# Chunk attention with a split-precision FFN: steps of the attention issued apart, spread evenly, new orders for tiles 2 and 3, aligned pools

## The chip, the cores and the metric

The kernel runs on one core of a Trainium2 chip. Its metric is the device time of one execution in microseconds (us). TensorE (PE) multiplies, VectorE (DVE) and ScalarE (ACT) do elementwise work and reductions, GpSimd (POOL) does some elementwise work too, and the queue of SyncE (SP) issues almost all DMAs. Each engine works through its own instructions in the order in which they were issued and waits on semaphores for the others.

## The reference

Attention within chunks of 64 positions for 8 x 8 heads of 576 positions of 64 features, then a layer norm, a feed-forward network with a ReLU, and a residual:

```python
def _attn_ref(q, k, v):                    # q, k, v: 8, 8, 576, 64
    q_c = q.reshape(B, H, nc, chunk, D)    # chunk = 64, nc = 9; k_c, v_c likewise
    scores = scale * np.matmul(q_c, k_c.transpose(0, 1, 2, 4, 3))
    scores = scores - np.max(scores, axis=-1, keepdims=True)
    attn = np.exp(scores)
    attn = attn / (np.sum(attn, axis=-1, keepdims=True) + 1e-09)
    return np.matmul(attn, v_c)

def _moe_ref(x, g_ln, w_ch1, w_ch2):       # x: 8, 576, 512; w_ch1: 512 x 2048; w_ch2: 2048 x 512
    mu = np.mean(x, axis=-1, keepdims=True)
    var = np.mean((x - mu) ** 2, axis=-1, keepdims=True)
    xn = (x - mu) / np.sqrt(var + 1e-06) * g_ln
    ch = np.maximum(xn @ w_ch1, 0.0) @ w_ch2
    return (x + ch).astype(np.float32)
```

All inputs are float32. The weights of the network reach the chip as 64-bit words and are rounded there.

## The kernel before

**Tokens.** The 4608 tokens form 18 pairs of 2 x 128 tokens, and two pairs form a tile of 512. Tiles 0 to 2 lead; tiles 3 to 8 are taken two at a time, in three units of 1024 tokens. Every wide product is made of three float32r products of a high and a low part (h and l), which stand in for float32: high by high, high by low, low by high.

**Attention of a pair** (`attention`) is a generator. Each `next` issues one step: load q and k, scores on TensorE into the one buffer of the pool `ps_a`, row maxima (`top`) and the load of v, subtraction (VectorE) and exp (ScalarE), four groups of 32x32 transposes on VectorE, denominators, the out product, scaling to x, statistics for the norm and its power -0.5 on POOL, the centred and weighted `xg` with its scaling by `rstd` on ScalarE, four groups of transposes into `rows`. With `by_pe` the transposes run on TensorE through a `ps_a` buffer. `p_sb`, `pt_sb`, `xg` take turns in two buffers of the pool `work`.

**Leading tiles** use the plain network (`ffn`): 16 features groups, each with a run of 12 matmuls up (`u`) and 12 down, a ReLU on ScalarE (`hh`) and its rest on VectorE (`hl`) between (`1`). The order for tile 1 and tile 2 is written out by hand: `SECOND` and `THIRD` give, for each position of the network's run, letters whose generators are stepped ahead of it. A and B are the pairs of tile 2, C and G those of tile 3, D and H those of tile 4, S the preparation of the weights' sums and parts for the units (POOL, ScalarE, DMAs to DRAM), P and Q the operands of the first unit for C with D and for G with H (`combine`), R the start of the ring of weight buffers.

**A unit** (`unit_ffn`) multiplies up by a seven-product scheme of sums: in each of four quarters 14 products of 6 matmuls, with snapshots copied by ScalarE (`snap`) and sums added by VectorE (`hu`), 336 matmuls in all. Then it multiplies down in two halves of 16 runs of 12 matmuls, 384 in all, each run with a relu (`hh` or `hx`) and a rest (`hl` or `hx`) of a later part. Two of five places of these parts lie in the pool `hp`, three (`hx`) in the pool `raws`. While units 0 and 1 run, `weave` steps the attention of the next unit's four pairs: after each `yield n` of the unit it counts n matmuls on and issues every side step that is due. The due counts come from `PAIR_SPAN`, `LOADED` and `STEPS` for the pairs and from `FIRST_HALF`, `LAST_HALF`, `ONE_STEP` for the operands of the next unit.

Nothing is reordered by a scheduler (`manual_schedule`): what is issued first stands first in its engine's queue. The joint step on which the prediction rests most:

```python
            nc.vector.tensor_tensor(out=p_b, in0=s4, in1=top4, op=ALU.subtract)
            nc.scalar.activation(p_sb, p_sb, AF.Exp, scale=scale)
        yield
```

Of the kernel before, what the change touches and what calls it, by code (L numbers as in the profile page):

```python
# [8 lines left out]
F32 = mybir.dt.float32  # L9
# [5 lines left out]
ALU = mybir.AluOpType  # L15
AX = mybir.AxisListType

P = 128
# [7 lines left out]
HP = H // 2  # L26
# [28 lines left out]
FIRST_HALF = 345  # L55
LAST_HALF = 585
REST = (2, 6, 12, 28)
# [34 lines left out]
def quad(i):  # L92
    return slice(32 * i, 32 * i + 32)
# [3 lines left out]
def chunk_attention_ffn(ctx: ExitStack, tc: tile.TileContext, qkv, v01, g, w, out):  # L97
# [9 lines left out]
    small = ctx.enter_context(tc.tile_pool(name="small", bufs=4))  # L107
    raws = ctx.enter_context(tc.tile_pool(name="raws", bufs=1))
# [8 lines left out]
    mhalf = const.tile([P, 2], F32, name="mhalf")  # L117
    nc.gpsimd.memset(mhalf, -0.5)
# [138 lines left out]
    def attention(pair, xt_cols, xs, by_pe, den_by_pe, rows_of=None):  # L257
# [60 lines left out]
        if den_by_pe:  # L318
            for h2 in range(2):
                nc.tensor.matmul(  # L320
                    s2[:, h2, :], lhsT=minus.bitcast(F32), rhs=top4[:, h2], start=False, stop=True,
                    skip_group_check=True,
                )
            nc.scalar.activation(p_b, s4, AF.Exp, scale=scale)
        else:
            nc.vector.tensor_tensor(out=p_b, in0=s4, in1=top4, op=ALU.subtract)  # L326
            nc.scalar.activation(p_sb, p_sb, AF.Exp, scale=scale)  # L327
# [5 lines left out]
        pt_sb = work.tile([P, groups, 2, D], F32, name="pt_sb", tag="work")  # L333
# [99 lines left out]
        for j in range(2):  # L433
            nc.vector.scalar_tensor_tensor(  # L434
                out=xg[:, j, :], in0=x[:, j, :], scalar=mv[:, j, 0:1], in1=g_sb, op0=ALU.subtract, op1=ALU.mult
            )
            if rows_of:
                nc.scalar.activation(xg[:, j, :], xg[:, j, :], AF.Copy, scale=rstd[:, j : j + 1])  # L438
        yield

        if rows_of:
            rows_t = rows_of()
            if by_pe:
                xt = halves()
                for j in range(2):
                    for k in range(NK):
                        ks = slice(k * P, (k + 1) * P)
                        nc.tensor.transpose(out=xt[j][:, ks], in_=xg[:, j, ks], identity=ident)
                    nc.scalar.copy(rows_t[:, :, j * P : (j + 1) * P], xt[j].rearrange("p (k t) -> p k t", k=NK))
                    yield  # L450
            else:
                to = rows_t.rearrange("p k (j t) -> p j k t", j=2)
                of = xg.rearrange("p j (k t) -> p j k t", k=NK)
                for j in range(4):
                    for i in range(4):
                        for h2 in range(2):
                            nc.vector.transpose(  # L457
                                out=to[quad(j), h2, :, quad(i)], in_=of[quad(i), h2, :, quad(j)]
                            )
                    yield  # L460
            return
# [242 lines left out]
    def rows_of(i):  # L704
        if "rows" not in shared:
            shared["rows"] = [xtp.tile([P, NK, 2 * PAIR], F32, name="rows", tag=f"xt{c}") for c in "hl"]
        return shared["rows"][i // 2][:, :, i % 2 * PAIR : (i % 2 + 1) * PAIR]
# [6 lines left out]
    def combine(half):  # L714
        cs = slice(half * PAIR, (half + 1) * PAIR)
        a, b = (r[:, :, cs] for r in shared["rows"])
        b11, b21, b12, b22 = a[:, :2], a[:, 2:], b[:, :2], b[:, 2:]

        def part(name, x):
            o = operand(name)  # L720
            nc.scalar.copy(o[:, 0, :, cs], x)  # L721
            nc.gpsimd.tensor_tensor(out=o[:, 1, :, cs], in0=x, in1=o[:, 0, :, cs].bitcast(F32), op=ALU.subtract)  # L722
# [24 lines left out]
        part("4", b21)  # L747
        yield

    def unit_ffn(u):  # L750
# [22 lines left out]

        def add(out, bank, s):
            nc.vector.tensor_tensor(out=out, in0=bank, in1=s, op=ALU.add)  # L775
# [5 lines left out]
        def split(i):  # L781
# [6 lines left out]
            nc.scalar.activation(hh, x, AF.Relu)  # L788
# [3 lines left out]
            parts.append((hh, hl))  # L792

        for q in range(NF // 4):
# [8 lines left out]

            for e in range(2):
                w0, w1 = pair_of()
                product(c_[e], w0, "2", True)
                yield 6
                product(a_[e], w1, "1", True)
                ring.fetch()
                nc.scalar.copy(s[e][0], a_[e])  # L810
                add(h[e][:, 0, 0], c_[e], s[e][0])
                yield 6
            for e in range(2):
                w0, w1 = pair_of()
                product(a_[e], w0, "6", False)
                nc.scalar.copy(s[e][1], a_[e])
                yield 6
                product(c_[e], w1, "5", True)
                ring.fetch()
                nc.scalar.copy(s[e][2], c_[e])  # L820
                yield 6
            for e in range(2):
                w0, w1 = pair_of()
                product(a_[e], w0, "7", False)
                add(h[e][:, 1, 1], a_[e], s[e][2])
                yield 6
                product(c_[e], w1, "3", False)
                ring.fetch()
                add(h[e][:, 1, 0], c_[e], s[e][1])
                if q == NF // 4 - 1:  # L830
                    split(e)
                yield 6
            w01 = pair_of()
            for e in range(2):
                product(a_[e], w01[e], "4", False)
                if e == 1:
                    ring.fetch()
                nc.scalar.copy(h[e][:, 0, 1], a_[e])  # L838
                yield 6
# [7 lines left out]
        for n in range(2):  # L847
# [3 lines left out]
            def down(f, w, j, m):  # L851
                hh, hl = (x[:, j * P : (j + 1) * P] for x in parts[n * NF + f])
# [7 lines left out]
            for f in range(NF):  # L860
                ws[f] = ring.take()[:, : 2 * DM].rearrange("p (h n) -> p h n", h=2)
                if f < NF - 2:
                    for m, j in [(m, j) for j in range(4) for m in range(3)] if f == 0 else [
                        (m, j) for m in range(3) for j in range(4)
                    ]:
# [10 lines left out]
                    yield 12  # L876
            for j in range(4):
                for f in range(NF - 2, NF):
                    for m in range(3):
                        down(f, ws[f], j, m)  # L880
                pair, jj = pairs[j // 2], j % 2
# [7 lines left out]
                if j == 3:  # L889
                    ring.fetch()  # L890
                    ring.fetch()
                    for f in range(NF - 2, NF):
                        if n * NF + f + ahead < 2 * NF:
                            split(n * NF + f + ahead)
                yield 6
# [18 lines left out]
    class Tokens:  # L914
# [10 lines left out]
        def attention(self, i, by_pe=False, den_by_pe=False):  # L925
# [3 lines left out]
            return attention(2 * self.t + i, lambda: self.cols(i), xs, by_pe, den_by_pe, rows)  # L929
# [14 lines left out]
    with tc.manual_schedule():  # L944
# [4 lines left out]
            G=tiles[3].attention(1), H=tiles[4].attention(1, True), S=prepare(), R=start_ring(), P=combine(0), Q=combine(1),  # L949
# [60 lines left out]
```

## Time and profile before

| | |
|---|---|
| median of three runs | 879.55 us (878.25 to 879.68) |
| the profiled execution | 880.14 us, of which the span of instructions is 878.3 us |
| mean granted clock of TensorE | 0.992 |
| busy: TensorE, VectorE, ScalarE, POOL | 843.6, 569.8, 270.3, 150.0 us |
| HBM | 147.08 MB read, 39.85 MB written |

The profile gives for every instruction its start, its length, the idle time of its engine before it and what ended that idle time. In its lines a group stands as line, engine, operation, written tile <- read tiles, shapes and count. In the order of time, a line begins with start and length in us, and the idle time before it with its releaser stands in brackets. The chain that ended last is the path, followed back from the last instruction, of what released what. Matmuls overlap, so the time that one takes in a run is the distance from start to start, not its own length of about 390 ns.

### The profile page before, as it was taken

Reading aid. Unit: us, or ns where it says so; the run is one execution under the profiler, and the core shown is the slowest. Engines: PE = TensorE matmul, PEld = TensorE weight load, DVE = VectorE, ACT = ScalarE, POOL = GpSimd, SP = SyncE. Lnnn points to the kernel's source line nnn. Section 1 sums busy time; section 2 is a strip of 40 time slices with the busy share of each in tenths; the row PEclk is TensorE's granted clock in tenths of the full one; section 3 lists DMA queues with packets and bytes.
Section 4 is the critical chain, followed back from the end, with each engine's and each line's share of the span. In section 5 each row is a group of like instructions: output and inputs, shape, how many; then the busy total and the mean of one; then the engine's idle time right before and its main releaser. Section 6 shows DMA issues by size and latency. Waiting matters only on the chain.

```text
span 878.3 us, 14775 instructions
## 1 busy us (share of the span) xinstructions
PE 843.6 (96%) x5850; PEld 686.8 (78%) x5850; DVE 569.8 (65%) x1101; ACT 270.3 (31%) x425; POOL 150.0 (17%) x138
## 2 busy tenths in 40 slices
PE   7999999999898899999998999999989999999998
PEld 4888888887677688878886888778868888888886
DVE  6989947567837734788987846879888622132321
ACT  5766321122322322232422412234322212232220
POOL 0110024473811122100120220001301300000000
PEclk9999999999999999999999999999999999999999
DMA  9996509948861046776783769767756776666573
GB/s 356 325 294 165 193 0 333 334 161 276 273 215 66 0 168 229 229 242 216 236 316 138 271 195 324 243 209 251 240 188 219 238 240 192 194 195 234 192 261 119
DMA packets 69044, 192.60 MB, mean 219 GB/s; under 512 B 6640, under 2 KB 20976, under 8 KB 67056
## 3 DMA queue, kind: packets, MB, share of 16 engines
q1 hardware_dynamic: 67680, 186.95, 62.7%
q0 software_dynamic: 1296, 4.72, 2.8%
q8 instruction: 46, 0.75, 0.3%
q14 instruction: 22, 0.18, 0.1%
HBM read 147.08 MB, written 39.85 MB: 213 GB/s over the span
## 4 chain that ended last, share of the span: by engine, by line
PE 75%; DVE 14%; issue 6%; DMA 2%; ACT 2%; POOL 1%; SPq 0%; ACTq 0%; POOLq 0%; DVEq 0%
PE y L769 22%; PE y L853 19%; PE y L543 11%; PE h L519 11%; PE h L853 8%; DVE rows L457 3%; DVE pt_sb L349 2%; PE s L294 1%; PE h L378 1%; DMA wp<-wfs 1%; DVE xg L434 1%; DVE p_sb L326 1%; DVE hu L775 1%; DVE stats L422 1%; DVE xt L492 1%
## 5 line engine op out<-in xcount | busy, mean ns | idle before, releaser
L769 PE MATMUL y<-xc,ring 128*128 128x512 f32 x1008 | 233.2, 391 | 2.7 <-ACT hu L838 2.0
L769 PEld LDWEIGHTS y<-xc,ring 128*128 128x128 f32 x1008 | 188.1, 188 | 43.9 <-ACT hu L838 2.8
L853 PE MATMUL y<-ring,hx 128*128 128x512 f32 x486 | 132.6, 400 | 1.5 <-ACT hx L788 1.5
L519 PE MATMUL h<-xth,wp 128*128 128x512 f32 (+1 forms) x432 | 130.1, 372 | 1.3 <-DMA wp<-wfs 1.3
L853 PEld LDWEIGHTS y<-ring,hx 128*128 128x128 f32 x486 | 91.6, 190 | 24.0 <-ACT hx L788 2.3
L775 DVE TENSOR_TENSOR hu<-y,snap 128x512 f32<-128x512 f32 x72 | 48.8, 688 | 82.9 <-ACT snap L810 50.8
L543 PE MATMUL y<-wp,hh 128*128 128x512 f32 x376 | 96.3, 394 | 0.0
L519 PEld LDWEIGHTS h<-xth,wp 128*128 128x128 f32 x432 | 79.0, 190 | 16.1 <-DMA wp<-wfs 1.5
L722 POOL TENSOR_TENSOR xc<-rows,xc 128x512 fp32r<-128x512 f32 x42 | 57.5, 1382 | 146.2 <-ACT xc L721 143.1
L349 DVE STREAM_TRANSPOSE pt_sb<-p_sb 32x256 f32<-32x256 f32 x176 | 76.7, 436 | 6.6 <-ACT p_sb L327 2.3
L543 PEld LDWEIGHTS y<-wp,hh 128*128 128x128 f32 x376 | 69.4, 189 | 14.0
L533 DVE SCALAR_TENSOR_TENSOR hl<-h,hh 128x512 fp32r<-128x512 f32 (+1 forms) x53 | 33.0, 628 | 72.4 <-ACT hh L532 71.9
L519 PE MATMUL h<-xtl,wp 128*128 128x512 f32 (+1 forms) x216 | 78.8, 369 | 0.0
L457 DVE STREAM_TRANSPOSE rows<-xg 32x128 f32<-32x128 f32 x288 | 71.6, 282 | 4.1 <-ACT xg L438 2.0
L853 PE MATMUL y<-ring,hh 128*128 128x512 f32 x252 | 71.8, 395 | 0.0
L789 DVE SCALAR_TENSOR_TENSOR hx<-hu,hx 128x512 fp32r<-128x512 f32 x54 | 41.7, 790 | 40.0 <-ACT hx L788 14.6
L532 ACT ACTIVATE hh<-h 128x512 fp32r<-128x512 f32 (+1 forms) x53 | 28.5, 545 | 106.6 <-PE h L519 102.3
L853 PEld LDWEIGHTS y<-ring,hh 128*128 128x128 f32 x252 | 47.7, 190 | 11.2 <-DVE hu L775 0.6
L543 PE MATMUL y<-wp,hl 128*128 128x512 f32 x188 | 51.8, 389 | 0.0
L853 PE MATMUL h<-ring,hx 128*128 128x512 f32 x162 | 50.9, 395 | 0.0
L428 POOL TENSOR_TENSOR rstd<-vare,mhalf 128x2 f32<-128x2 f32 x12 | 10.8, 901 | 230.3 <-DVE vare L427 230.3
L788 ACT ACTIVATE hx<-hu 128x512 fp32r<-128x512 f32 x54 | 33.1, 628 | 48.9 <-PE y L853 29.8
(129 smaller groups left out, 1005.1 us busy)
## 6 DMA issues: line engine op xcount, KB each, us to landing
ring<-w2d SPq DMA_DIRECT2D x96, 512.0 KB, 4.2
ring<-wa SPq DMA_DIRECT2D x84, 512.0 KB, 4.3
raw<-w SPq DMA_DIRECT2D x15, 1024.0 KB, 7.4
out<-x SPq DMA_DIRECT2D x36, 256.0 KB, 4.4
q_t<-qkv SPq DMA_DIRECT2D x17, 512.0 KB, 6.1
k_t<-qkv SPq DMA_DIRECT2D x17, 512.0 KB, 6.9
v_t<-qkv SPq DMA_DIRECT2D x32, 256.0 KB, 6.8
w2d<-wp SPq DMA_DIRECT2D x16, 512.0 KB, 7.3
```

What stands on the lines that cost most here:

```text
L349: nc.vector.transpose(out=pt_sb[quad(2 * h2 + j), :, c, quad(i)], in_=p_sb[quad(2 * c + i), :, h2, quad(j)])
L457: nc.vector.transpose(out=to[quad(j), h2, :, quad(i)], in_=of[quad(i), h2, :, quad(j)])
L519: nc.tensor.matmul(h, lhsT=(wh, wh, wl)[m][:, ks], rhs=(xth, xtl, xth)[m][:, k, :], start=i == 0, stop=i == len(terms) - 1,)
L532: nc.scalar.activation(hh, h, AF.Relu)
L533: nc.vector.scalar_tensor_tensor(out=hl, in0=h, scalar=0.0, in1=hh.bitcast(F32), op0=ALU.max, op1=ALU.subtract)
L543: nc.tensor.matmul(sums(pairs[j // 2])[j % 2], lhsT=(hh, hh, hl)[m], rhs=(wh, wl, wh)[m], start=f == 0 and m == 0, stop=f == NF - 1 and m ...
L722: nc.gpsimd.tensor_tensor(out=o[:, 1, :, cs], in0=x, in1=o[:, 0, :, cs].bitcast(F32), op=ALU.subtract)
L769: nc.tensor.matmul(bank, lhsT=w[:, (0, 0, 1)[m], ks], rhs=x[:, (0, 1, 0)[m], k, :], start=start and k == m == 0, stop=k == 1 and m == 2, s ...
L775: nc.vector.tensor_tensor(out=out, in0=bank, in1=s, op=ALU.add)
L788: nc.scalar.activation(hh, x, AF.Relu)
L789: nc.vector.scalar_tensor_tensor(out=hl, in0=x, scalar=0.0, in1=hh.bitcast(F32), op0=ALU.max, op1=ALU.subtract)
L853: nc.tensor.matmul(ys[j], lhsT=(hh, hh, hl)[m], rhs=w[:, (0, 1, 0)[m]], start=f == 0 and m == 0, stop=f == NF - 1 and m == 2,)
```

## The change

- Subtraction and exp become two steps where the rows go to a unit, and so do `xg` and its scaling. In the unit, relu (`split`) and rest (`rest`) are issued at different places within a run, a run of 12 matmuls yields three times instead of once, and in the product stage the side steps are issued ahead of a product's fetch, copies and adds instead of behind them.
- `rows` is laid out by token half first, so that a group of transposes is 4 of 32x256 instead of 8 of 32x128; `combine` reads and writes it with strides.
- `STEPS` has 18 entries for 16, `PAIR_SPAN` is 140 for 138; `SECOND`, `THIRD`, `ROOMS` and `REST` are new. H's `pt_sb` lies in the pool `raws`.
- `mhalf` is 128 bytes wide instead of 8, and a pool of 64 bytes lies ahead of `raws`.

```diff
 SECOND = {
-    0: "ABS", 1: "AS", 2: "AS", 3: "AS", 4: "A", 5: "AS", 6: "AS", 7: "ABS", 8: "AS", 9: "AC", 10: "AS", 11: "AS",
-    12: "AS", 13: "AS", 14: "A", 15: "AS", 16: "BS", 17: "BS", 18: "BS", 19: "B", 20: "BS", 21: "BS", 22: "BS",
-    23: "BCS", 24: "BC", 25: "BBS", 26: "BS", 27: "BBS", 28: "BBS", 29: "CD", 30: "CCS", 31: "CS", 32: "C",
+    0: "ABS", 1: "AS", 2: "S", 3: "AAS", 4: "AS", 5: "AAS", 6: "S", 7: "AS", 8: "AAS", 9: "AAS", 10: "AAS", 11: "BAS",
+    12: "BAC", 13: "BS", 14: "S", 15: "BBS", 16: "BS", 17: "BBS", 18: "S", 19: "BS", 20: "BBCS", 21: "BBS", 22: "BBDS",
+    23: "BCS", 24: "BC", 25: "CS", 26: "S", 27: "CCS", 28: "CS", 29: "CCS", 30: "CDS", 31: "CDDS", 32: "DS",
 }
 THIRD = {
-    0: "CDS", 1: "CDS", 2: "DGS", 3: "CS", 4: "CDDS", 5: "DS", 6: "DS", 7: "DG", 8: "DG", 9: "GH", 10: "DGG", 11: "DGG",
-    12: "GP", 13: "GHP", 14: "GHP", 15: "GGP", 16: "GGHP", 17: "GGP", 18: "P", 19: "HHP", 20: "HP", 21: "HHP", 22: "HP",
-    24: "H", 25: "H", 26: "QQ", 27: "QQR", 28: "Q", 29: "QXXN", 30: "QR",
+    0: "CS", 1: "CS", 2: "DDG", 3: "D", 4: "DD", 5: "D", 6: "DG", 7: "GGH", 8: "DG", 9: "D", 10: "GGP", 11: "HGP",
+    12: "GGP", 13: "GHP", 14: "GGHP", 15: "GHP", 16: "GP", 17: "HHGP", 18: "HGG", 19: "HGP", 20: "HP", 21: "HP",
+    22: "H", 24: "H", 25: "H", 26: "QQ", 27: "QR", 28: "Q", 29: "QXXN", 30: "QQR", 31: "Q",
 }
-ROOMS = {1: (3, 11), 2: (6,)}
-PAIR_SPAN = 138
+ROOMS = {1: (3, 9), 2: (6,)}
+PAIR_SPAN = 140
-STEPS = (0, 8, 16, 30, 40, 50, 60, 70, 80, 87, 95, 105, 116, 126, 136, 146)
-ONE_STEP = 8
+STEPS = (0, 6, 11, 18, 26, 37, 48, 59, 68, 76, 88, 95, 102, 110, 118, 129, 140, 158)
+ONE_STEP = 9
-LAST_HALF = 585
-REST = (2, 6, 12, 28)
+LAST_HALF = 592
+REST = (2, 6, 20)
...
+    gap = ctx.enter_context(tc.tile_pool(name="gap", bufs=1))
+    gap.tile([P, 16], F32, name="gap")
     raws = ctx.enter_context(tc.tile_pool(name="raws", bufs=1))
...
-    mhalf = const.tile([P, 2], F32, name="mhalf")
+    halves_ = const.tile([P, 32], F32, name="mhalf")
+    mhalf = halves_[:, :2]
...
             nc.vector.tensor_tensor(out=p_b, in0=s4, in1=top4, op=ALU.subtract)
+            if rows_of:
+                yield
             nc.scalar.activation(p_sb, p_sb, AF.Exp, scale=scale)
...
-            if rows_of:
+        yield
+        if rows_of:
+            for j in range(2):
                 nc.scalar.activation(xg[:, j, :], xg[:, j, :], AF.Copy, scale=rstd[:, j : j + 1])
-        yield
+            yield
...
-                to = rows_t.rearrange("p k (j t) -> p j k t", j=2)
-                of = xg.rearrange("p j (k t) -> p j k t", k=NK)
+                to = rows_t.rearrange("p j k t -> p (j k) t")
+                of = xg.rearrange("p j (k t) -> p (j k) t", k=NK)
                 for j in range(4):
                     for i in range(4):
-                        for h2 in range(2):
-                            nc.vector.transpose(
-                                out=to[quad(j), h2, :, quad(i)], in_=of[quad(i), h2, :, quad(j)]
-                            )
+                        nc.vector.transpose(out=to[quad(j), :, quad(i)], in_=of[quad(i), :, quad(j)])
                     yield
...
             nc.scalar.activation(hh, x, AF.Relu)
+            parts.append((hh, hl, x))
+
+        def rest(i):
+            hh, hl, x = parts[i]
             nc.vector.scalar_tensor_tensor(
...
+            for i, (bank, e, name, then) in enumerate(steps):
+                if i % 2 == 0:
+                    w01 = pair_of()
+                product(bank[e], w01[i % 2], name, name in "215")
                 yield 6
+                if i % 2:
                     ring.fetch()
+                if then:
+                    then(e)
+                if q == NF // 4 - 1 and name in "34":
+                    (split if name == "3" else rest)(e)
...
                         down(f, ws[f], j, m)
+                        if at % 4 == 3:
+                            yield 4
+                            if at == 3 and n == f == 0:
+                                rest(2)
+                            if at == 3 and f > 0 and i - 1 < 2 * NF:
+                                split(i - 1)
+                            if at == 7 and f > 0 and i - 1 < 2 * NF:
+                                rest(i - 1)
                     ring.fetch()
-                    if n * NF + f + ahead < 2 * NF:
-                        split(n * NF + f + ahead)
...
+                yield 6
                 pair, jj = pairs[j // 2], j % 2
                 x = back[pair][:, jj, :]
                 nc.vector.tensor_tensor(out=x, in0=ys[j], in1=x, op=ALU.add)
...
+                if n == 0 and j < 3:
+                    split(NF + j)
+                    rest(NF + j)
```

`then` holds the copies and adds of a product as before (`copy` and `add`; the products keep their order), and `i` in the down stage is the number of the part three runs ahead.

More of the change, by code (lines that the diff above doesn't have):

```diff
@@ L255, in unspill, with attention @@
         return x
-    def attention(pair, xt_cols, xs, by_pe, den_by_pe, rows_of=None):
+    def attention(pair, xt_cols, xs, by_pe, den_by_pe, rows_of=None, pt_raw=False):
         if pair == 1:
@@ L331, in attention @@
             nc.gpsimd.memset(v_1.rearrange("p j a b d -> p (j a b) d")[:, :, D:], 1.0)
-        pt_sb = work.tile([P, groups, 2, D], F32, name="pt_sb", tag="work")
+        if pt_raw:
+            pt_sb = raws.tile([P, groups, 2, D], F32, name="pt_raw", tag="wf")
+        else:
+            pt_sb = work.tile([P, groups, 2, D], F32, name="pt_sb", tag="work")
         if by_pe:
@@ L772, in product, with copy @@
                     )
+        def copy(out, bank):
+            nc.scalar.copy(out, bank)
         def add(out, bank, s):
@@ L802, in pair_of @@
                 return w[:, 0], w[:, 1]
+            steps = []
             for e in range(2):
-                w0, w1 = pair_of()
-                product(c_[e], w0, "2", True)
-                yield 6
[L808 to L836, printed above, removed]
+                steps += [
+                    (c_, e, "2", None),
+                    (a_, e, "1", lambda e: (copy(s[e][0], a_[e]), add(h[e][:, 0, 0], c_[e], s[e][0]))),
+                ]
@@ new lines, in unit_ffn @@
+            for e in range(2):
+                steps += [
+                    (a_, e, "6", lambda e: copy(s[e][1], a_[e])),
+                    (c_, e, "5", lambda e: copy(s[e][2], c_[e])),
+                ]
+            for e in range(2):
+                steps += [
+                    (a_, e, "7", lambda e: add(h[e][:, 1, 1], a_[e], s[e][2])),
+                    (c_, e, "3", lambda e: add(h[e][:, 1, 0], c_[e], s[e][1])),
+                ]
+            for e in range(2):
+                steps += [(a_, e, "4", lambda e: copy(h[e][:, 0, 1], a_[e]))]
@@ L851, in down @@
             def down(f, w, j, m):
[L852 removed]
+                hh, hl = (x[:, j * P : (j + 1) * P] for x in parts[n * NF + f][:2])
                 nc.tensor.matmul(
@@ L888, in unit_ffn @@
                     stores.append((out[row : row + P, :], x))
[L889 to L895, printed above, removed]
+                if n == 0 and j < 3:
+                    split(NF + j)
+                    rest(NF + j)
+            ring.fetch()
+            ring.fetch()
         for to, of in stores:
```

34 lines of the change are left out of this document (16 added, 18 removed).

## The prediction

> **What bounds the kernel now.** I read the page first, then the busy times by stage (the stages are cut where the chain that ended last goes from one loop to the next), the chain itself, and the order of time on TensorE, ScalarE and VectorE around each gap.
>
> ```profile
> PE 843.6 (96%) x5850; PEld 686.8 (78%) x5850; DVE 569.8 (65%) x1101; ACT 270.3 (31%) x425; POOL 150.0 (17%) x138
> ```
> ```profile
> 0.00:132.00 132.00, 124.12 (x1147) 101.76 (x1147) 106.21 (x153) 72.06 (x97) 13.73 (x24) 1.00 0.68 222
> 132.00:218.00 86.00, 86.00 (x619) 71.24 (x616) 58.24 (x109) 18.49 (x26) 44.02 (x40) 1.00 0.82 282
> 218.00:342.00 124.00, 112.38 (x910) 91.44 (x909) 72.94 (x136) 34.28 (x57) 42.41 (x37) 0.97 0.43 150
> ...
> 526.00:710.00 184.00, 178.27 (x1232) 143.88 (x1232) 143.88 (x321) 53.00 (x90) 23.52 (x18) 0.99 0.70 235
> 710.00:875.00 165.00, 164.56 (x719) 134.64 (x717) 43.73 (x65) 38.47 (x64) 0.00 (x0) 1.00 0.64 208
> ```
>
> Columns behind the stretch and its length: busy time of PE, PEld, DVE, ACT, POOL, then granted clock, DMA share, GB/s. TensorE is the bound, so only its idle time, its clock and the time between its matmuls can be won. The stage of tile 1 (132 to 218) has no idle time. The stage of tile 2 (218 to 342) has 124 - 112.38 = 11.62 us of it at a clock of 0.97. A unit with attention beside it (526 to 710; the unit ahead of it is like it) has 184 - 178.27 = 5.73 us at 0.99. The last unit, with no side work, has nearly none.
>
> The chain gives the price of a clean unit:
>
> ```profile
> 525.55 2.72 PE y L769 x12
> 528.26 1.09 PE s L294 x64
> 529.36 17.91 PE y L769 x78
> ...
> 709.74 76.16 PE y L769 x336
> 785.90 45.71 PE y L853 x198
> ...
> 874.60 0.69 DVE x L883
> ```
>
> Unit 2 runs from 525.55 to 709.74, 184.2 us; unit 3, with the same 720 wide matmuls, to 874.60, 164.9 us. Four pairs of attention add eight blocks of 64 small matmuls; a block takes 1.09 and makes the run behind it 17.91 - 78 x 0.2267 = 0.23 longer, so 8 x 1.32 = 10.6. The other 184.2 - 164.9 - 10.6 = 8.7 us of a unit are waits and what follows from them.
>
> These are the waits of unit 2, in order of time on TensorE, with the granted clock around the worst:
>
> ```profile
> 566.61 5.74 PE L769 MATMUL y<-xc,ring 128*128 128x512 f32 x24 [0.38 <-DVE hu L775]
> 573.33 1.90 PE L769 MATMUL y<-xc,ring 128*128 128x512 f32 x7 [0.98 <-ACT hu L838]
> 646.94 5.86 PE L853 MATMUL y<-ring,hx 128*128 128x512 f32 x24 [0.76 <-ACT hx L788]
> 656.14 0.30 PE L378 MATMUL h<-v_t,pt_sb 64*64 64x64 f32 x2 [3.07 <-DVE pt_sb L349]
> 656.97 1.50 PE L378 MATMUL h<-v_t,pt_sb 64*64 64x64 f32 x58 [0.54 <-DVE pt_sb L349]
> ```
> ```profile
> 646.00:666.00 20.00, 15.63 (x117) 12.27 (x117) 16.26 (x32) 4.24 (x8) 0.00 (x0) 0.91 0.34 113
> ```
>
> They add up to the 5.73. And what stood in front, on ScalarE and VectorE:
>
> ```profile
> 569.23 1.22 DVE L301 TENSOR_REDUCE top<-s 128x16 f32<-128x1024 f32 x1
> 570.49 1.22 DVE L326 TENSOR_TENSOR p_sb<-s,top 128x1024 f32<-128x1024 f32 x1
> 573.80 0.69 DVE L775 TENSOR_TENSOR hu<-y,snap 128x512 f32<-128x512 f32 x1 [2.08 <-ACT snap L810]
> ```
> ```profile
> 571.75 1.06 ACT L327 ACTIVATE p_sb<-p_sb 128x1024 f32<-128x1024 f32 x1 [4.90 <-DVE p_sb L326]
> 572.71 0.57 ACT L838 COPY hu<-y 128x512 f32<-128x512 f32 x1
> ...
> 645.31 1.06 ACT L327 ACTIVATE p_sb<-p_sb 128x1024 f32<-128x1024 f32 x1 [8.85 <-DVE p_sb L326]
> 646.28 1.66 ACT L788 ACTIVATE hx<-hu 128x512 fp32r<-128x512 f32 x3
> ```
>
> Subtraction and exp of a pair are issued in one step. ScalarE then stands 4.90 (later 8.85) us at the exp, waiting for a late VectorE, and the copy that frees TensorE's bank, or three relus that make its operands, stand behind it. VectorE in turn waits for those copies (2.08), so its lag lasts, until a pair's out product at 653 finds its transposes missing.
>
> **The change, part by part.** The profiled execution took 880.14 us (span 878.3); the median is 879.55, 0.6 less, and the gain is taken from the median.
>
> *Aligned pools.* In the program as allocated, tiles are rounded up to 32 bytes and pools lie one behind the other; every large tile but those of the pool "raws" starts 32 bytes over a multiple of 128, those of raws 96 over. The wider mhalf (32 to 128 bytes) and the gap of 64 bytes put all of them on multiples of 128. What the 96 costs is seen where the operand's parts lie in raws (hx) and where they don't (hh, hl):
>
> ```profile
> 802.32 1.98 PE L853 MATMUL y<-ring,hh 128*128 128x512 f32 x8
> 804.14 1.07 PE L853 MATMUL y<-ring,hl 128*128 128x512 f32 x4
> 805.04 8.56 PE L853 MATMUL y<-ring,hx 128*128 128x512 f32 x36
> 813.44 1.78 PE L853 MATMUL y<-ring,hh 128*128 128x512 f32 x7
> ```
> ```profile
> 6.05 1.30 PE L235 MATMUL y<-minus 128*128 128x512 f32 x5
> ```
>
> From start to start, hx takes (813.44 - 805.04) / 36 = 233 ns, hh and hl (805.04 - 802.32) / 12 = 227. Over a unit: 45.71 / 198 = 230.9 against 76.16 / 336 = 226.7, so 4.2 ns x 384 = 1.6 us, 4.8 in three units. The value for "all on 128" is not in the main loops; the nearest row is the keep-warm run, where both operands are minus, on a multiple of 128: (1.30 - 0.39) / 4 = 228 with a last matmul of 0.39 as elsewhere, so 227 is not expected to move. Ends: 0 and 4.8. I take 4.8, as the difference follows the pool.
>
> A rule speaks against it: the Trainium skill (SBUF — State Buffer, Specifications) has lines of 16 bytes and a penalty for each new line; 32 and 96 are both multiples of 16, so by it this part gives nothing. The hx row differs all the same.
>
> *Units 1 and 2.* Subtraction and exp, xg and its scaling, relu and its rest become steps 6 to 8 matmuls (1.4 to 1.8 us) apart, so the second engine no longer stands at the first one's queue; a pair gets 140 matmuls for 138, the side steps come ahead of a product's copies instead of behind. The row transposes go from 32 small to 16 larger:
>
> ```profile
> L349 DVE STREAM_TRANSPOSE pt_sb<-p_sb 32x256 f32<-32x256 f32 x176 | 76.7, 436 | 6.6 <-ACT p_sb L327 2.3 <-PE s L448 1.7
> L457 DVE STREAM_TRANSPOSE rows<-xg 32x128 f32<-32x128 f32 x288 | 71.6, 282 | 4.1 <-ACT xg L438 2.0
> ```
>
> 32 x 71.6/288 = 8.0 becomes 16 x 76.7/176 = 7.0: 1.0 us a pair, 4 us of VectorE's 143.9 in a unit. That itself is off the path; it shortens the lag. In the second half of a unit a part's relu is now issued 20 matmuls (4.5 us) ahead of its use instead of 24; the tightest, the last part of a half, 11 (2.5 us), for a relu of 0.55 and a rest of about 0.69, which I count as covered; uncovered it costs up to 1.2 a half. Of a unit's 8.7 I take 6.5: of the 5.73 named, 4.7 (about one us of the out product's wait stays, as its last transposes are now issued 17 matmuls ahead instead of 20), and of the remaining 3.0, most of which follows the pauses (clock 0.91 for 20 us is 1.8), 1.8. Two units: 13. Ends: 17.5, and a loss where the copies behind the side steps come late (third rival).
>
> *The orders of tiles 2 and 3.* The six waits of 218 to 342:
>
> ```profile
> 219.87 1.09 PE L338 MATMUL s<-ident,p_sb 128*128 128x128 f32 x8 [1.47 <-ACT p_sb L327]
> ...
> 240.37 0.63 PE L448 MATMUL s<-ident,xg 128*128 128x128 f32 x4 [3.13 <-DVE p_sb L326]
> ...
> 246.56 1.09 PE L338 MATMUL s<-ident,p_sb 128*128 128x128 f32 x8 [0.79 <-ACT rows L449]
> ...
> 278.32 1.60 PE L378 MATMUL h<-v_t,pt_sb 64*64 64x64 f32 x58 [2.29 <-DVE hl L533]
> ...
> 300.89 1.10 PE L338 MATMUL s<-ident,p_sb 128*128 128x128 f32 x8 [2.42 <-ACT p_sb L327]
> ...
> 306.26 1.16 PE L378 MATMUL s<-v_t,pt_sb 64*64 64x64 f32 x64 [1.52 <-ACT pt_sb L340]
> ```
>
> They are the whole 11.62. By the order's positions, each a run of mostly 12 matmuls (2.72 us): C's exp and its transposes stood one apart, now two. D's subtraction stood one position ahead of C's row transposes, which need its bank; it stands two runs behind the scores now. C's second transposes and D's first shared a position and a bank; now one apart. G's four transposes came in two positions, with D's row transposes between; now three runs lie between the first and the out product, 8.2 us and a block of 1.3, for VectorE's 4 x 4 x 0.436 = 7.0 and one hl: tight, I leave 1.0. H's exp leaves G's row transposes and gets two positions (pt_raw gives its transposes room of their own). H's out still follows one run behind, so 1.5 stays. That removes 9.1; of the clock's 0.03 x 124 = 3.7 I take 2.0. Against it, tile 1's stage takes over steps of C and D and five more steps of the weight preparation (31 for 26); it has no idle time but little room in transfers (0.82 busy, so about 0.9): 1.6 lost. Net 9.5. Ends: +15.3, and -5 if tile 1's stage stalls as this one did.
>
> *At nothing:* the rows' new layout, whose strided reads meet instructions such as
>
> ```profile
> L722 POOL TENSOR_TENSOR xc<-rows,xc 128x512 fp32r<-128x512 f32 x42 | 57.5, 1382 | 146.2 <-ACT xc L721 143.1
> ```
>
> with POOL busy 23.52 of 184 in a unit; slower by half they would add 14 x 0.7 = 10 us to POOL in a unit, under matmuls, unless the last parts are late for the next unit. The fetches keep their number and are issued a run's end later, with five of six places still ahead. The last unit has no side work, and nothing else moves there.
>
> Sum: 4.8 + 13 + 9.5 = 27.3; 879.55 - 27.3 = 852.
>
> **The rivals.**
>
> *The lag stays.* VectorE is still busy about 140 of 175 us in a unit, the weight preparation and the row steps still meet, and half the waits come back at other steps: 4.8 + 4 + 5 = 13.8, so 866. For it: the out product's cover shrinks from 20 to 17 matmuls. Against: the exp rows, where ScalarE's 4.90 and 8.85 come from the joint issue.
>
> *Alignment does nothing* (233 is due to something else about hx): 857.
>
> *Slower: copies behind the side steps.* A snapshot copy now follows a step such as the exp; its bank is wanted 12 matmuls after its product, 2.72 us, less 0.57 for the copy and 1.06 for the exp: 1.1 us to spare. If VectorE is as late as at 569.23 (the scores were done at 563.2, six us before), each of three exps in the product stage holds TensorE some 5 us, 30 in two units, less the 2.7 paid there now; with 14.3 from the other parts, 892. It decides from a lag of about 4 us on. Against: that very lag cost only 0.98 + 0.38 there.
>
> *All matmuls speed up.* If 227 is itself the price of the 32 bytes, as 233 is of the 96, another 6 ns on some 3,240 wide matmuls gives 19 us more: 833. The keep-warm row speaks against it. For it, the Trainium skill (TensorE: Matmul & The Clock Gate, "Wait — 56ns, not 53.3ns?") has 215.7 ns for this width, which no row here reaches; by it the gain would be an estimated 36 us.
>
> *All waits go:* 4.8 + 17.5 + 15.3, so 842. *The edits cancel:* 880.
>
> **How the numbers follow.** Forecast 0.50; alignment nothing 0.15; lag stays 0.17; slower 0.06; all speed up 0.03; all waits go 0.05; cancel 0.04. The range 845 to 867 holds the first three, 0.82. A measurement of this kernel tells 0.2% (1.8 us) from no change; faster is 0.90, same 0.04, slower 0.06.
>
> **What would show it.** Right: hx at 227 ns from start to start; units 1 and 2 at about 176 us with a clock of 1.00; exps that wait under 2 us on VectorE and no relu stacked behind them; under 3 us idle on TensorE from 218 to 342. Wrong: snapshot or relu releasers with more than 5 us in TensorE's waits, stalls in tile 1's stage, or an out product still waiting 3 us in each unit.

## The result, and the profile after

The changed kernel takes 853.07 us (median of four, 852.65 to 853.97) against 879.08 (four of before): a ratio of 0.9706 with a 95% interval of 0.9689 to 0.9723. The profiled execution took 852.65 us and its span of instructions is 850.9 us, so the span is 27.4 us shorter than before.

The page's busy times and the stages after (columns as in the prediction; the cuts follow the loops):

```profile
PE 836.7 (98%) x5850; PEld 682.4 (80%) x5850; DVE 563.1 (66%) x957; ACT 271.1 (32%) x425; POOL 150.7 (18%) x138
```
```profile
130.00:216.00 86.00, 85.35 (x730) 70.06 (x723) 62.53 (x115) 21.15 (x30) 54.73 (x49) 1.00 0.85 297
216.00:329.00 113.00, 111.42 (x856) 90.64 (x856) 66.02 (x116) 32.47 (x53) 34.59 (x31) 1.00 0.43 152
...
506.00:683.00 177.00, 175.78 (x1234) 142.86 (x1233) 142.44 (x257) 53.31 (x90) 23.59 (x18) 1.00 0.73 244
683.00:847.00 164.00, 164.00 (x719) 134.60 (x717) 43.05 (x64) 38.50 (x64) 0.00 (x0) 1.00 0.63 208
```

TensorE's idle time in tile 2's stage fell from 11.62 to 1.58 us and in unit 2 from 5.73 to 1.22, and the granted clock is 1.00 in each. What TensorE still waits for in the whole kernel (us in total, number of times, the longest):

```profile
PE y L239 <- ACT minus L958: 2.4, 1, 2.4
PE y L860 <- DVE hl L804: 2.3, 4, 0.9
PE s L298 <- ACT p_sb L328: 1.1, 1, 1.1
PE s L298 <- DMA k_t<-qkv: 1.0, 1, 1.0
PE s L459 <- ACT rows L460: 0.8, 1, 0.8
PE y L239 <- DVE x L407: 0.7, 1, 0.7
PE h L387 <- DVE hl L541: 0.7, 1, 0.7
PE h L527 <- DVE x L421: 0.5, 1, 0.5
...
PE h L387 <- DVE pt_sb L358: 0.3, 1, 0.3
```

(Line 860 is the down product of a unit, 387 the out product, 459 a row transpose, 527 the up product.) The waits at lines 239 and 298 lie in the first 25 us, where the change does nothing; the kernel before has them too. Of the waits that the prediction names for the units and for tile 2's stage, none is left; the largest still there is that of the down product for a late rest, up to 0.9 us at a time. The chain that ended last shows the units; unit 2 takes 176.9 us for 184.2:

```profile
505.70 2.72 PE y L777 x12
...
682.56 76.16 PE y L777 x336
758.72 45.61 PE y L860 x198
```

The 45.61 tells something else: before it was 45.71, so the matmuls with hx are hardly faster. Of the 27.4 us, 14.7 came in units 1 and 2, 0.3 in unit 3, 12.4 ahead of the units, of it 1.5 in the first 55 us, where the change alters no instruction, only addresses (last section).

For the experiments the table holds, beside the timed ratio, the start of the first unit and three lengths from each profile's order of time. Units 1 and 2 are taken from the first product of one unit to that of the next, unit 3 to the start of its last matmul; these lengths do not depend on what happens in the first 55 us.

| kernel | median us | ratio to before (95%) | first unit starts | unit 1 | unit 2 | unit 3 |
|---|---|---|---|---|---|---|
| before | 879.08 | 1 | 341.2 | 184.2 | 184.2 | 164.6 |
| changed | 853.07 | 0.9706 (0.9689 to 0.9723) | 328.8 | 176.8 | 176.9 | 164.4 |
| unaligned | 853.71 | 0.9726 (0.9704 to 0.9747) | 328.3 | 176.9 | 177.0 | 164.6 |
| gap of 192 bytes | 849.59 | 0.9680 (0.9658 to 0.9701) | 327.6 | 176.1 | 176.1 | 163.0 |
| gap of 448 bytes | 852.56 | 0.9701 (0.9675 to 0.9727) | 331.8 | 176.0 | 176.1 | 163.0 |
| old orders | 862.81 | 0.9828 (0.9806 to 0.9850) | 338.8 | 176.7 | 177.2 | 164.3 |
| joint exp | 852.77 | 0.9697 (0.9680 to 0.9714) | 328.4 | 176.8 | 176.9 | 164.3 |
| joint relu and rest | 852.83 | 0.9699 (0.9676 to 0.9722) | 329.9 | 176.4 | 176.5 | 164.4 |
| small transposes | 856.16 | 0.9741 (0.9718 to 0.9764) | 329.2 | 178.1 | 178.1 | 164.4 |
| side steps behind | 856.50 | 0.9735 (0.9713 to 0.9757) | 329.5 | 179.0 | 178.3 | 164.3 |
| old counts | 853.56 | 0.9720 (0.9696 to 0.9744) | 329.9 | 177.0 | 177.1 | 164.3 |
| new counts alone | 874.45 | 0.9953 (0.9938 to 0.9967) | 337.8 | 181.6 | 182.9 | 164.6 |
| joint, old counts | 855.04 | 0.9731 (0.9709 to 0.9753) | 329.0 | 177.8 | 178.1 | 164.4 |
| gap, early rests | 849.92 | 0.9667 (0.9648 to 0.9686) | 329.1 | 175.9 | 176.0 | 163.0 |

Each ratio is to runs of the kernel before that were made beside it. Their medians were 879.08 us for the changed kernel, 877.27 for the next four rows, 879.80 for the four from "joint exp" on and 879.25 for the last four. So medians of different groups can't settle differences of about 2 us, and the lengths, each from one profiled execution, are used for those.

### The profile page after: what moved, and what is told of

It is laid out like the page before. It is cut to its first block, busy times and chain, and to the rows that moved or that the text cites. A ratio compares the mean times of both kernels' runs of the same rounds, so it can differ in the third digit from the quotient of the medians.

```text
span 850.9 us, 14618 instructions
## 1 busy us (share of the span) xinstructions
PE 836.7 (98%) x5850; PEld 682.4 (80%) x5850; DVE 563.1 (66%) x957; ACT 271.1 (32%) x425; POOL 150.7 (18%) x138
## 4 chain that ended last, share of the span: by engine, by line
PE 78%; DVE 15%; issue 2%; POOL 2%; ACT 1%; DMA 1%; SPq 0%; POOLq 0%; ACTq 0%; DVEq 0%
PE y L777 24%; PE y L860 14%; PE h L527 14%; PE y L551 13%; PE h L860 8%; DVE pt_sb L358 4%; DVE rows L467 3%; PE s L298 2%; DVE hx L804 1%; DVE hl L804 1%; DVE den L365 1%; DVE xt L500 1%; PE s L387 1%; DMA k_t<-qkv 1%; PE h L387 1%
## 5 line engine op out<-in xcount | busy, mean ns | idle before, releaser
L860 PE MATMUL y<-ring,hx 128*128 128x512 f32 x486 | 130.7, 396 | 0.0
L783 ACT COPY snap<-y 128x512 f32<-128x512 f32 x72 | 42.2, 587 | 121.8 <-PE y L777 121.8
L467 DVE STREAM_TRANSPOSE rows<-xg 32x256 f32<-32x256 f32 x144 | 62.7, 435 | 5.4 <-ACT xg L449 3.2
L551 PE MATMUL y<-wp,hl 128*128 128x512 f32 x188 | 51.8, 390 | 0.0
```

The lines of the kernel that those rows point to most:

```text
L467: nc.vector.transpose(out=to[quad(j), :, quad(i)], in_=of[quad(i), :, quad(j)])
L551: nc.tensor.matmul(sums(pairs[j // 2])[j % 2], lhsT=(hh, hh, hl)[m], rhs=(wh, wl, wh)[m], start=f == 0 and m == 0, stop=f == NF - 1 and m ...
L783: nc.scalar.copy(out, bank)
L860: nc.tensor.matmul(ys[j], lhsT=(hh, hh, hl)[m], rhs=w[:, (0, 1, 0)[m]], start=f == 0 and m == 0, stop=f == NF - 1 and m == 2,)
```

## The experiments

**Alignment: undone, and two other gaps.** The first takes the change's alignment out again, the others move raws a little further.

```diff
-    gap = ctx.enter_context(tc.tile_pool(name="gap", bufs=1))
-    gap.tile([P, 16], F32, name="gap")
...
-    halves_ = const.tile([P, 32], F32, name="mhalf")
+    halves_ = const.tile([P, 2], F32, name="mhalf")
```

> The changed kernel without the wider mhalf and without the gap, so raws starts 96 and all else 32 bytes over a multiple of 128, as before the change. If the alignment of the change is worth what the prediction gave it, 4.8 us are lost: 857.9. If it is worth what the traces of before and after show (233.3 against 232.5 ns a matmul with hx, 648 of them), 0.5 us: 853.5. It also tells whether the first 54 us, 1.4 us shorter in the trace after, owe that to the addresses.

```diff
-    gap.tile([P, 16], F32, name="gap")
+    gap.tile([P, 48], F32, name="gap")
```

> The changed kernel with a gap of 192 bytes for 64, so raws starts at the same place within 512 bytes as all other large tiles (256 over a multiple of 512; with the gap of 64 it is 128 over). Theory 'phase': a matmul is slow where its stationary and its moving operand lie at different places within 256 or 512 bytes, whatever their own alignment: hx falls from 232.5 to 227 ns, 1.2 us a unit, 3.6 in all: 849.5. Rival 'region': the upper end of the memory, where raws lies, is slow to read as stationary operand: no change, 853. Rival 'alignment to 128': no change, 853.

```diff
-    gap.tile([P, 16], F32, name="gap")
+    gap.tile([P, 112], F32, name="gap")
```

> The changed kernel with a gap of 448 bytes: raws starts at the same place within 256 bytes as the others, but not within 512 (0 over a multiple of 512, the others 256). If the phase counts within 256 bytes: hx at 227 ns and 849.5, as with 192. If it counts within 512: hx stays at 232 or more, 853. Region: 853.

TensorE's order of time in unit 3, the same stretch of hh, hl and hx, in the changed kernel, unaligned, with 192 and with 448 bytes:

```profile
775.09 1.98 PE L860 MATMUL y<-ring,hh 128*128 128x512 f32 x8
776.91 1.08 PE L860 MATMUL y<-ring,hl 128*128 128x512 f32 x4
777.82 8.53 PE L860 MATMUL y<-ring,hx 128*128 128x512 f32 x36
786.19 1.98 PE L860 MATMUL y<-ring,hh 128*128 128x512 f32 x8
```
```profile
774.96 1.98 PE L858 MATMUL y<-ring,hh 128*128 128x512 f32 x8
776.77 1.07 PE L858 MATMUL y<-ring,hl 128*128 128x512 f32 x4
777.68 8.56 PE L858 MATMUL y<-ring,hx 128*128 128x512 f32 x36
786.07 2.00 PE L858 MATMUL y<-ring,hh 128*128 128x512 f32 x8
```
```profile
775.02 8.32 PE L860 MATMUL y<-ring,hx 128*128 128x512 f32 x36
783.18 1.98 PE L860 MATMUL y<-ring,hh 128*128 128x512 f32 x8
```
```profile
779.18 8.32 PE L860 MATMUL y<-ring,hx 128*128 128x512 f32 x36
787.34 1.98 PE L860 MATMUL y<-ring,hh 128*128 128x512 f32 x8
```

From start to start over 36 matmuls: 8.37 us (232.5 ns) as changed, 8.39 (233.1) unaligned, 8.16 (226.7) with either gap. By the sizes of the tiles in the program (the traces hold no addresses), the moving operand (ring) lies, within 256 bytes, 64 away from hx before and unaligned, 128 away as changed, and at the same place with 192 and with 448 bytes. So in these runs it is not an operand's own alignment that counts: hx on a multiple of 128 takes 232.5 ns, hh and hl of the unaligned kernel, 32 over one, take (777.68 - 774.96) / 12 = 226.7. What counts is whether both operands lie at the same place within 256 bytes; within 512 isn't needed. The region theory falls: raws is still the last pool. The group "last" of tile 2, also in raws, points the same way: about 234 ns as changed, 226.7 with either gap. Taken alone the alignment of the change is worth 0.6 us in the three units together (518.5 us unaligned, 518.0 as changed). The gap of 192 takes another 2.8 off them; its median is 3.5 lower, near the 3.6 expected, but the two medians come from different groups. In the first 55 us the unaligned kernel is within 0.3 us of the changed one, so by these profiles the 1.5 us there are not owed to the addresses. The median with 448 bytes lies 3 us over that with 192 although the units are as short; its runs stand in two groups (848.9 and 849.1; 852.6 to 853.6), and its profile shows where (last section).

**The old orders of tiles 2 and 3.**

```diff
-SECOND = { ... }, THIRD = { ... }, ROOMS = {1: (3, 9), 2: (6,)}, REST = (2, 6, 20)    # as changed
+SECOND = { ... }, THIRD = { ... }, ROOMS = {1: (3, 11), 2: (6,)}, REST = (2, 6, 12, 28)    # as before
...
-            if rows_of:
+            if rows_of and not joint:      # joint for C, D, G, H: subtraction with exp, xg with its scaling
                 yield
```

> The changed kernel with the orders of tiles 2 and 3 from before (the positions, the rooms, the rest of Q in the first unit, and for the pairs C, D, G, H the joint steps and pt_sb in its old pool); units 2 and 3 as changed. By the prediction's terms 9.5 us come back: 862.6. By the traces (to the first unit 341.4 before, 328.9 after, of it 1.4 in the first 54 us) 11: 864. Rival: the two parts overlap (a late VectorE at the end of this stage would also cost in the first unit): more than 13, 866 or over.

862.81, 9.7 over the median of the changed kernel. In the profiles the first unit starts 10.0 us later (338.8 for 328.8), with the first 55 us alike. The waits of before are back, at the same places (view of waits, TensorE):

```profile
PE s L347 <- ACT p_sb L333: 3.4, 2, 1.9
PE s L461 <- DVE p_sb L330: 3.1, 1, 3.1
...
PE h L387 <- DVE hl L543: 2.3, 1, 2.3
...
PE s L387 <- ACT pt_sb L349: 1.0, 1, 1.0
PE s L347 <- ACT rows L462: 0.8, 1, 0.8
```

The units stay at 176.7 and 177.2, so the two parts of the change add up and do not overlap. This run undoes the positions together with the joint steps of the pairs C, D, G and H, so it does not tell how much of the 10 us belongs to which.

**The units: each part undone alone.** First the joint issue, which the prediction took for the cause:

```diff
-STEPS = (0, 6, 11, 18, 26, 37, 48, 59, 68, 76, 88, 95, 102, 110, 118, 129, 140, 158)
+STEPS = (0, 6, 11, 26, 37, 48, 59, 68, 76, 88, 95, 102, 118, 129, 140, 158)
...
-            streams[u, n] = tiles[LEAD + 2 * u + n % 2].attention(n // 2)
+            streams[u, n] = tiles[LEAD + 2 * u + n % 2].attention(n // 2, joint=True)
```

> The changed kernel, but in units 1 and 2 subtraction and exp are one step again, and xg and its scaling (the due counts 18 and 110 are taken out, all others stay; tiles 2 and 3 as changed). Theory 'queue head' (the prediction's): ScalarE standing at an exp or a scaling with copies and relus behind it made most of the waits of units 1 and 2, which the change cut by 7.4 us a unit: 4 or more come back in each, 861 to 866, with copies (hu, snap) or relus (hx) as releasers. Rival 'less work on VectorE and even spacing': the joint issue costs under 1 a unit, 853 to 855.

The units take 176.8 and 176.9, as changed. ScalarE does wait again at the exps; the waits of before, of the changed kernel and of this one, in that order:

```profile
ACT p_sb L327 <- DVE p_sb L326: 51.8, 14, 8.9
```
```profile
ACT p_sb L333 <- DVE p_sb L330: 15.0, 6, 3.9
```
```profile
ACT p_sb L333 <- DVE p_sb L330: 41.0, 12, 8.2
```

41.0 us of waiting for 15.0, up to 8.2 at a time, and no time lost: what stood behind the exp had room enough. For the changed kernel, queue head in its strong form is refuted.

```diff
-                            if at == 3 and f > 0 and i - 1 < 2 * NF:
-                                split(i - 1)
-                            if at == 7 and f > 0 and i - 1 < 2 * NF:
-                                rest(i - 1)
...
+                    if i < 2 * NF:
+                        split(i)
+                        rest(i)
...
+                    yield 12       # for three yields of 4
```

> The changed kernel, but relu and rest of a part are issued together at the end of a run, three runs ahead, as before the change, and the side steps get one place in a run instead of three. Queue head: VectorE stands at a rest whose relu waits behind other work of ScalarE, so 1 to 2 us a unit: 855 to 857. Rival: the relus have 24 matmuls of cover instead of 20, nothing is lost, 853, or up to 1 us a unit won at the start of the down stage, where the rest is now late by 0.9.

852.83, the units 0.3 and 0.4 shorter than as changed, in one profile each: the rival was right, nothing is lost, and this part of the change may cost a little. The medians do not show it.

```diff
-                        nc.vector.transpose(out=to[quad(j), :, quad(i)], in_=of[quad(i), :, quad(j)])
+                        for h2 in range(2):
+                            ks = slice(h2 * NK, (h2 + 1) * NK)
+                            nc.vector.transpose(out=to[quad(j), ks, quad(i)], in_=of[quad(i), ks, quad(j)])
```

> The changed kernel with the row transposes as 32 of 32x128 instead of 16 of 32x256 (same layout): VectorE gets about 1.0 us more for a pair, 4 us a unit. Queue head: VectorE has room (142 of 177 us busy in a unit), so at most 1 us a unit, 853 to 855. Rival 'less work': the lag comes from VectorE's load in the attention's stretch, so half of the 7.4 us a unit comes back, 860.

856.16, 1.2 to 1.3 us a unit: over the "at most 1" of the one theory, under half of what the other asked.

```diff
                 product(bank[e], w01[i % 2], name, name in "215")
-                yield 6
                 ...                # fetch, copies, adds
+                yield 6
```

> The changed kernel with the side steps issued behind a product's fetch, copies and adds (and behind the final adds and relus of a half), as before the change. Queue head: copies no longer stand behind side steps, but side steps of VectorE stand behind adds that wait for the product just issued, so they run a product (1.4 us) later: out products wait longer, 0 to 2 us a unit, 853 to 857. The prediction's slower rival turned round would have it faster than 853.

856.50, 1.5 to 2.2 us a unit, the largest of the four. TensorE's order of time names the place:

```profile
599.42 0.29 PE L387 MATMUL h<-v_t,pt_sb 64*64 64x64 f32 x2 [0.95 <-DVE pt_sb L358]
600.25 1.14 PE L387 MATMUL h<-v_t,pt_sb 64*64 64x64 f32 x58 [0.54 <-DVE pt_sb L358]
```

An out product waits for its transposes again. VectorE began that pair's transposes 80.4 us into the unit, as changed 78.6. That this comes from the adds ahead of the side steps, which wait for the product just issued, is argued from the order of issue; no run shows it by itself. The prediction's slower rival, that copies behind side steps cost more than they bring, has the wrong sign.

**The due counts.**

```diff
-PAIR_SPAN = 140
+PAIR_SPAN = 138
...
-STEPS = (0, 6, 11, 18, 26, 37, 48, 59, 68, 76, 88, 95, 102, 110, 118, 129, 140, 158)
+STEPS = (0, 8, 16, 23, 30, 40, 50, 60, 70, 80, 87, 95, 105, 111, 116, 126, 136, 146)
...
```

> The changed kernel with the due counts of before (138 matmuls a pair; steps at 0, 8, 16, 23, 30 ... 146, the two new steps halfway; operand steps every 8, the second half from 585). Undone one at a time, joint exp gave 0, joint relu and rest -0.4, small transposes 1.3 and side steps behind 1.8 us a unit, 2.7 of 7.4. Theory 'spacing': the even due counts are the rest: 4 or more a unit, 861 or over. Rival 'redundant parts': each part alone is enough cover, so this too costs under 2 a unit, up to 856.5.

Undone in the changed kernel, 0.2 to 0.3 a unit (853.56): "spacing" as the missing part is refuted, and what "redundant parts" expected came true here. The other way round, in the kernel before:

```diff
-PAIR_SPAN = 138
+PAIR_SPAN = 140
...
-STEPS = (0, 8, 16, 30, 40, 50, 60, 70, 80, 87, 95, 105, 116, 126, 136, 146)
+STEPS = (0, 6, 11, 26, 37, 48, 59, 68, 76, 88, 95, 102, 118, 129, 140, 158)
...
```

> The kernel before with nothing changed but the due counts (140 a pair; 0, 6, 11, 26, 37 ... 158; operand steps every 9, the second half from 592), with its joint steps. Spacing: a unit of 184.2 us falls by 4 or more, 867 to 871. Redundant parts: also 4 or more, as one part alone gives most of the cover. Rival 'queue head': the joint exps and the late VectorE stay, under 2 a unit, 875 or over.

874.45, with units 2.6 and 1.3 us shorter: less than the 4 or more that spacing and redundant parts both asked, and about what queue head asked. So "redundant parts" fails in this direction: one part alone does not give most of the cover. In unit 2 the granted clock is 0.98, before it was 0.99, which takes back part of the 2.1 us that no longer stand idle there. The copies and relus no longer hold TensorE, although exp and subtraction are joint, but the out product does:

```profile
647.55 0.30 PE L378 MATMUL h<-v_t,pt_sb 64*64 64x64 f32 x2 [2.99 <-DVE pt_sb L349]
648.38 1.97 PE L378 MATMUL h<-v_t,pt_sb 64*64 64x64 f32 x58 [0.54 <-DVE pt_sb L349]
```

So the two kinds of wait in a unit of before have different causes: 2.1 us at copies and relus, which even counts alone remove, and 3.6 us at one out product, which they don't. Joint issue and old counts, both back in the changed kernel (e9 is the run with the old counts):

> The changed kernel with both: subtraction and exp, xg and scaling joint again in units 1 and 2, and the due counts of before. Queue head in its weaker form (a joint exp costs only where VectorE lags, and it lags with the old counts): 2 or more a unit over e9. Rival: the same as e9 within 0.5 a unit, and the joint issue is shown to cost nothing in either spacing.

```diff
-STEPS = (0, 6, 11, 18, 26, 37, 48, 59, 68, 76, 88, 95, 102, 110, 118, 129, 140, 158)
+STEPS = (0, 8, 16, 30, 40, 50, 60, 70, 80, 87, 95, 105, 116, 126, 136, 146)
...
-            streams[u, n] = tiles[LEAD + 2 * u + n % 2].attention(n // 2)
+            streams[u, n] = tiles[LEAD + 2 * u + n % 2].attention(n // 2, joint=True)
```

855.04: 0.8 to 0.9 a unit over the old counts alone, between both expectations. In these runs joint issue costs something only with the uneven counts. ScalarE's wait at the exps shows how little such a wait says about the time:

```profile
ACT p_sb L333 <- DVE p_sb L330: 53.8, 12, 9.8
```

That is more than the 51.8 us of before, in units of 177.8 and 178.1 us for 184.2.

**A version made from this.** The gap of 192 bytes, and the two waits on a rest that are left in a unit attacked:

```diff
-                    (split if name == "3" else rest)(e)
+                    name == "3" and (split(e), rest(e))
...
+                if n == 0 and j < 3:       # ahead of the final add, not behind it
+                    split(NF + j)
+                    rest(NF + j)
```

> The changed kernel with the gap of 192 bytes, with the rests of the first two parts issued with their relus at product 3 of the last quarter instead of behind product 4, and with the relus and rests of the second half's first parts ahead of the first half's final adds. The gap gives 849.6 as before; the two waits on a rest (1.06 and 0.3 to 0.5 a unit) go, 2.5 to 3 in two units: 846.8. Rival: the earlier rests push the transposes of the third pair back and the out product waits instead: 849.6.

849.92, units of 175.9 and 176.0 for 176.1 and 176.1 with the gap alone: the rival was right. The wait on hl went from 2.6 us with the gap alone to 0.8, and out products (0.9 for 0.3) and products (0.4 for none) wait instead. The gap alone, 849.59, is the best kernel here together with this one; they can't be told apart.

## Why the prediction was right, and where not

That the forecast of 852 came so near to 853.07 is luck in part, since misses of its sum cancelled. By the profiles the alignment gave 4.2 us less than its term, units 1 and 2 about 1.4 more than theirs, tiles 2 and 3 another 1.4 more, and 1.5 came in the first 55 us, where the change does nothing.

*Aligned pools, 4.8 predicted.* This is the step that failed. Measured: 0.25 us in unit 3 (164.6 to 164.4), 0.6 in the three units together (unaligned against changed). The reading of the rows (hx 233 against 227, worth 1.6 a unit) was right, and the gap of 192 bytes collects it: 164.4 to 163.0. The inference was wrong: I took the difference of the pools for a difference of alignment, and used the keep-warm run as a witness that a multiple of 128 gives 227. In that run both operands are the same tile, hence at the same place; by the rows with the gaps it would give 227 wherever that tile lies. So the rival that alignment does nothing had this part right, though not its time of 857, as the other parts gave more. The Trainium skill's rule on lines of 16 bytes (SBUF — State Buffer, Specifications) was nearer in its outcome, nothing, than my step, but by it 192 bytes would have given nothing either, and they took 2.8 us off the three units.

*Units 1 and 2, 13 predicted.* Measured 14.7, of it 0.5 or less from hx. Size right, reason mostly wrong. I had two places in the trace where ScalarE stood at an exp with a copy or relus behind (4.90 and 8.85 us), and took standing for costing. Undoing the joint issue raised that standing from 15.0 to 41.0 us and cost under 0.1 us a unit. Undone one at a time, the parts give per unit: joint exp 0.0, relu and rest -0.4, small transposes 1.2 to 1.3, side steps behind 1.5 to 2.2, old counts 0.2 to 0.3; together some 3 of 7.4. The other 4.4 belong to no part alone; which combination gives them is not shown. One part undone leaves most of the gain, but one part alone, the new counts in the kernel before, brings only 1.3 to 2.6. The prediction gave the transposes no price of their own (off the path, shortens the lag): undone, their 4 us of VectorE's work cost over 1 us a unit. What removes the 3.6 us at one out product of each unit stays open too. New counts alone leave it whole, and joint issue with old counts does not bring it back. That leaves the transposes (with the new layout of `rows`, which no run undid), the place of the side steps and that of relu and rest. Undone alone they bring back none, some 1.5 and 0.5 us a unit of the waits of out products; two of them together were not undone.

*Tiles 2 and 3, 9.5 predicted.* Undoing it cost 10.0 us in the profiles, and the waits that came back are the six that were named, H's out product with 1.0 for 1.5. From before to after this stretch gained 12.4 - 1.5 = 10.9; the other 0.9 is assigned to nothing. Against the list: C's, D's, G's and H's waits went; the 1.5 left for H's out product went too: before, ScalarE waited 2.77 us at a copy of P ahead of H's own copies, as changed P's copy is done first. D's wait of 0.79 went as counted, but C's second row transposes now wait as long, 0.8, for the bank's copy. Tile 1's stage pays 0.65 us idle (86 - 85.35, an out product behind a late hl) instead of the 1.6 I allowed.

*What would show it.* Units of 176 us at a clock of 1.00 and under 3 us idle in tile 2's stage came true. hx at 227 did not. The sign "exps that wait under 2 us and no relu stacked behind them" did not come true either: the trace after has an exp that waits 3.9 us with relus behind it, and TensorE loses nothing there.

## What to carry to other kernels

A wait on an engine that isn't the bound is no cost until the bound engine's own waits name what stands behind it: undo the one suspect before building on it. Several parts of one change can cover the same lag. Then they can't be priced one by one: here undoing each alone accounts for some 3 of 7.4 us a unit, and adding one alone brought 1.3 to 2.6. Where a matmul's distance from start to start differs between operands of the same shape, compare the places of both operands within 256 bytes, not one operand's alignment.

## What the runs showed of the hardware that I had not expected

The place of the stationary operand against the moving one, within 256 bytes, sets the distance between wide float32r matmuls: 226.7 ns at the same place, 232.5 at 128 bytes off, 233.1 to 233.3 at 64 off. Other distances were not tried, and why the place matters is not shown.

Between 47 and 55 us from the start, with all DMA engines busy, a transfer into a weight's low part (wp<-wfs) comes up to 2.2 us late for TensorE in some executions and not at all in others, in kernels that do not differ there in more than addresses. The stretch from 44 to 52 us in the run with 192 bytes and in that with 448 (columns as in the prediction):

```profile
44.00:52.00 8.00, 8.00 (x71) 7.10 (x72) 7.83 (x13) 6.51 (x11) 1.76 (x2) 1.00 1.01 323
```
```profile
44.00:52.00 8.00, 5.98 (x36) 5.41 (x35) 5.94 (x10) 4.84 (x8) 0.89 (x1) 0.87 1.00 320
```

The idle 2.0 us are followed by a clock of 0.87, and the first unit starts at 331.8 instead of 327.6. This is what separates the two groups of that kernel's runs as far as its one profile shows. A wait there does not always lower the clock: in the run with the old counts it takes 2.2 us, and the clock from 44 to 52 us is 1.00. The profile of before had such a wait of 1.3 us at 54 us, that of the changed kernel none, which accounts for most of the 1.5 us of the gain that the change did not make. What makes the transfer late was not tried.
